# Attention pairs of a fused kernel: raw queries loaded to both halves of the partitions, earlier loads, and another order of sixteen block moves

## The chip, the core and the metric

The program runs on one NeuronCore of one Trainium2 chip. Its time is device microseconds (us) for the whole program, one launch. Three executions of the kernel before gave 1097.83, 1100.74 and 1102.21 us, so the median is 1100.74. The profiled execution took 1099.78 us.

## The reference

Three stages follow each other. Only the first one is touched by the change.

```python
def _attn_ref(q, k, v):                       # 4 batches x 8 heads, S = 1152, D = 64
    q_pool = q.reshape(B, H, S // 2, 2, D).mean(axis=3)      # 576 pooled queries
    scores = scale * np.matmul(q_pool, k.transpose(0, 1, 3, 2))
    scores = scores - np.max(scores, axis=-1, keepdims=True)
    attn = np.exp(scores)
    attn = attn / (np.sum(attn, axis=-1, keepdims=True) + 1e-09)
    return np.matmul(attn, v)
# then _moe_ref  (576 x 512 tokens: w_k 512x1024, w_v 1024x512, w_r 512x512)
# then _moe2_ref (w_theta, w_tok_r, w_tok_i, w_ch)
```

The inputs are float32, except that the weights of the two later stages arrive as float64 and are converted on the chip.

## The kernel before

**Pairs and slots.** The 32 heads are worked off as 16 pairs P of two heads (h = 0 and 1). A pair has nine slots, one for each tile of at most 128 pooled queries against 1152 keys (the fifth tile, called None in the code, takes the last 64 queries of both heads). A slot makes the scores of the tile two slots ahead on TensorE (L304), takes their maximum on VectorE (L325, or L320 by thirds in the first pair), the exponential on ScalarE (L337), turns the result so that keys lie on partitions, and runs a share of the products with the values (L418, called PV below).

**Two cuts of one number.** Scores are formed to nearly float32 accuracy with numbers cut into a high and a low float32r part. GpSimd makes these cuts for the pair after the running one: `k_hi` (kh), four `k_lo` (kl), and for the queries `q_sum`, `q_scale`, `q_hi`, `q_lo` (the sum of two neighbouring queries, the scale 1/16, the high and the low part). TensorE's 128 rows hold key parts of one head: the high part in the head's own 64 partitions and the low part in the other 64. So the query parts of each head must stand in both halves of the partitions. Before, the cut queries of both heads (128 partitions) are moved there by four DMAs from SBUF to SBUF at the end of `q_lo` (L254), into the buffers Q12. The high key part moves by two DMAs (`k_move`, L268).

**Two ways to turn.** For pairs 1 to 14 the first four slots are turned in 32 x 32 blocks on VectorE (`turn_blocks`, L372, into the tile BLK). When the fourth is done, `move_blocks` (L380) puts the blocks in place with sixteen DMAs, from partitions 32a.. of BLK to partitions 32m.. of the tile E. One moves 144 KB. The first PV products that read E run in the eighth slot. The other five slots are turned on TensorE (L347) and copied by ScalarE and VectorE (L403).

**Weight conversion.** Beside this, 20 pieces of float64 weights are converted. A piece is loaded (L123, 512 KB), ScalarE takes a magnitude (L127), GpSimd clamps (L130), VectorE puts bits together in three steps, ScalarE and GpSimd cut (L146, L150), and two DMAs store (L154, L155). With a the slot of the first bit step, the load stands in slot a-6, the magnitude in a-3 and the clamp in a-2.

**What sets the order.** The order on each engine is written out by hand: `at_gap`, `at_mid` and `at` put a step at the start, in the middle or at the end of a slot (hooks 0, 1, 2). The table PREP lists (slot, hook, step, arguments) for the preparation of pair P during pair P-1 (PREP1 for P = 1). Steps whose name begins with l are loads, for pair P+1. All DMAs go out from SyncE's (SP's) queue in program order, so a DMA that waits for something holds up every DMA behind it. The tile pools give buffers in turn and add the waits. Raw queries, raw keys and high key parts have two buffers each (pool nat), E and BLK one.

Of the kernel before, what the change touches and what calls it, by code (L numbers as in the profile page):

```python
# [48 lines left out]
PREP1 = ((-1, 2, 'qs', 'pool'), (1, 0, 'kh', 'pool'), (1, 2, 'km'), (1, 2, 'kl', 'pool', 0, 0), (1, 2, 'kl', 'pool', 0, 1), (2, 2, 'qx', 'pool'), (2, 2, 'qh', 'pool'), (2, 2, 'ql', 'pool'), (3, 2, 'kl', 'pool', 1, 0), (4, 2, 'kl', 'pool', 1, 1), (5, 0, 'lqk'), (15, 2, 'lv'))  # L49
PREP = ((-1, 2, 'qs', 'pool'), (0, 0, 'kh', 'pool'), (0, 1, 'km'), (0, 1, 'qx', 'pool'), (0, 2, 'qh', 'pool'), (1, 1, 'ql', 'pool'), (2, 1, 'kl', 'pool', 0, 0), (3, 1, 'kl', 'pool', 0, 1), (4, 1, 'kl', 'pool', 1, 0), (5, 1, 'kl', 'pool', 1, 1), (7, 0, 'lqk'), (16, 0, 'lv'))  # L50
# [13 lines left out]
def attn_moe_kernel(ctx: ExitStack, tc: tile.TileContext, qT, kT, vP, muk, mur, wk, wv, wr, wth, wtr, wti, wch, ident, out):  # L64
# [94 lines left out]
    def attention(first):  # L159
# [73 lines left out]
        def q_sum(P, e):  # L233
            q = raws[P][0]
            engines[e].tensor_tensor(q[:, 0], q[:, 0], q[:, 1], ALU.add)  # L235

        def q_scale(P, e):
            q = raws[P][0]
            if e == "act":
                act.activation(q[:, 0], q[:, 0], AF.Copy, scale=1.0 / 16.0)  # L240
            else:
                engines[e].tensor_scalar(q[:, 0], q[:, 0], 1.0 / 16.0, 1.0, op0=ALU.mult, op1=ALU.mult)

        def q_hi(P, e):
            q = raws[P][0]
            cut_hi(e, q[:, 1].bitcast(F32R), q[:, 0])

        def q_lo(P, e):
            q = raws[P][0]
            cut_lo(e, q[:, 0], q[:, 0], q[:, 1])  # L250
            Q = Q12[P % 2]
# [3 lines left out]
            for h in range(2):
                d = slice(64 * h, 64 * h + 64)
                c = 512 * (1 - h)
                cut_hi("pool", QC[P % 2][d, d], q[d, 0, c:c + 64])
# [237 lines left out]
        steps = {
            "qs": q_sum, "qx": q_scale, "qh": q_hi, "ql": q_lo, "kh": k_hi, "kl": k_lo, "km": k_move,
            "lqk": load_qk, "lv": load_v,
        }

# [680 lines left out]
```

## Time and profile before

| what | value |
|---|---|
| median of three executions | 1100.74 us |
| profiled execution | 1099.78 us |
| its span, first to last instruction | 1098.0 us |
| pairs 0 to 15 | about 8.7 to 603 us of the span |
| TensorE busy | 957.4 us (87%) |
| VectorE / ScalarE / GpSimd busy | 694.3 / 515.7 / 528.1 us |
| mean granted TensorE clock | 0.941 |
| moved by DMA | 159.20 MB |

The two later stages, from about 603 us on, keep TensorE busy nearly all the time; in the pairs it waits. A view of waits lists an engine and line, what it waited for, the total in us, how often and the longest. A row of the timeline is start, duration, engine, line, operation, output and inputs, count, and in brackets the idle time before it with what ended it. The view of windows gives for each stretch its length, each engine's busy time with its count of instructions, TensorE's granted clock as a share of 2.4 GHz, the mean busy share of the 16 DMA engines and what they moved.

### The profile page before, as it was taken

The numbers are of one execution on the slowest core, as the hardware profiler recorded it, in microseconds if no ns is written. First come the engines' busy times: TensorE is split into PE (matmuls) and PEld (weight loads), VectorE is DVE, ScalarE is ACT, GpSimd is POOL, SyncE is SP. The second block draws the span as 40 slices with busy tenths as digits, with TensorE's granted clock in tenths as the row PEclk, the third lists the DMA queues.
The fourth block names the chain that finished last, engine by engine and source line by source line (L and its number), as shares of the span: only waits on it lengthen the run. The fifth ranks groups of instructions, "written<-read, shape, count | busy, mean of one in ns | idle before, by whom it ended". The sixth has DMA issues, their size and how long they took to land.

```text
span 1098.0 us, 17551 instructions
## 1 busy us (share of the span) xinstructions
PE 957.4 (87%) x6328; PEld 809.4 (74%) x6328; DVE 694.3 (63%) x1006; ACT 515.7 (47%) x1101; POOL 528.1 (48%) x571
## 2 busy tenths in 40 slices
PE   8686985796787687679689999999999999999998
PEld 6554664564555464556457899999999999999998
DVE  7485764675765575575445478888873676366631
ACT  7364444454545454454346555555554444244320
POOL 7415523532542453355135156566654665566641
PEclk9898987897988898898889999999999999999999
DMA  5777768768767777786671923333341240000011
GB/s 156 208 199 191 213 178 205 227 195 204 203 193 222 192 213 204 199 226 167 188 189 66 340 94 107 99 97 93 103 132 64 85 165 17 28 23 23 1 44 44
DMA packets 69927, 159.20 MB, mean 145 GB/s; under 512 B 12176, under 2 KB 31312, under 8 KB 69840
## 3 DMA queue, kind: packets, MB, share of 16 engines
q1 hardware_dynamic: 69840, 158.07, 50.8%
q8 instruction: 50, 0.82, 0.3%
q14 instruction: 37, 0.30, 0.1%
HBM read 73.08 MB, written 24.79 MB: 89 GB/s over the span
## 4 chain that ended last, share of the span: by engine, by line
PE 50%; issue 5%; SPq 4%; DMA 4%; DVE 4%; ACT 2%; POOL 1%; POOLq 0%; ACTq 0%; DVEq 0%
PE ps L1073 10%; PE ps L825 8%; PE ps L806 8%; PE pv L418 5%; PE ps L1092 5%; PE ps L1019 5%; PE sc L304 4%; SPq L380 3%; PE ps L775 2%; PE sc L347 2%; DMA cv<-wv 1%; DMA a<-wk 1%; DMA a<-wth 1%; DVE m L325 1%; PE ps L977 1%
## 5 line engine op out<-in xcount | busy, mean ns | idle before, releaser
L304 PE MATMUL sc<-kt,q 128*128 128x384 f32 (+1 forms) x864 | 214.7, 373 | 74.4 <-ACT M L403 62.5
L325 DVE TENSOR_REDUCE m<-sc 128x1 f32<-128x1152 f32 x138 | 187.1, 1356 | 113.9 <-PE sc L304 107.6
L304 PEld LDWEIGHTS sc<-kt,q 128*128 128x128 f32 (+1 forms) x864 | 151.7, 198 | 108.4 <-ACT M L403 66.1
L337 ACT ACTIVATE e<-sc,m 128x1152 f32<-128x1152 f32 x144 | 176.5, 1226 | 83.7 <-DVE m L325 79.6
L418 PE MATMUL pv<-E,vn 128*64 128x256 f32 x576 | 84.6, 436 | 51.9 <-DMA scr<-rt 50.1
L235 POOL TENSOR_TENSOR qn<-qn 128x576 f32<-128x576 f32 x15 | 21.3, 1417 | 199.5 <-DMA qn<-qT 145.6
L1073 PE MATMUL ps<-b,a 128*128 128x288 f32 x816 | 111.3, 296 | 0.0
L1073 PEld LDWEIGHTS ps<-b,a 128*128 128x128 f32 x816 | 109.4, 188 | 0.6
L403 DVE COPY M<-sc 128x384 f32<-128x384 f32 x77 | 41.8, 546 | 99.8 <-PE sc L347 99.7
L806 PE MATMUL ps<-x,a 128*128 128x288 f32 x768 | 103.7, 295 | 1.0 <-DVE xt L830 1.0
L418 PEld LDWEIGHTS pv<-E,vn 128*64 128x64 f32 x576 | 43.9, 153 | 80.9 <-issue 67.5
L825 PE MATMUL ps<-k,b 128*128 128x288 f32 x768 | 103.5, 295 | 0.0
L806 PEld LDWEIGHTS ps<-x,a 128*128 128x128 f32 x768 | 102.2, 188 | 1.4 <-DVE xt L830 1.3
L825 PEld LDWEIGHTS ps<-k,b 128*128 128x128 f32 x768 | 102.1, 188 | 0.3
L201 POOL TENSOR_TENSOR kt<-kn,kh 64x576 fp32r<-64x576 f32 (+1 forms) x64 | 93.2, 1472 | 3.1
L347 PEld LDWEIGHTS sc<-idn,e 128*128 128x128 f32 x528 | 67.5, 157 | 35.3 <-issue 17.6
L347 PE MATMUL sc<-idn,e 128*128 128x128 f32 x528 | 86.6, 307 | 6.7 <-ACT e L337 5.8
L403 ACT COPY M<-sc 128x384 f32<-128x384 f32 x83 | 39.3, 479 | 108.9 <-PE sc L347 108.5
L418 PE MATMUL pv<-M,vn 128*64 128x320 f32 x576 | 87.5, 440 | 0.0
L372 DVE STREAM_TRANSPOSE blk<-e 128x1152 f32<-128x1152 f32 x56 | 76.6, 1368 | 0.0
L793 POOL TENSOR_TENSOR k<-h,k 128x288 fp32r<-128x288 f32 x64 | 56.7, 901 | 18.7 <-ACT k L792 17.6
L418 PEld LDWEIGHTS pv<-M,vn 128*64 128x64 f32 x576 | 37.3, 136 | 36.1 <-issue 11.3
(136 smaller groups left out, 1604.3 us busy)
## 6 DMA issues: line engine op xcount, KB each, us to landing
E<-blk SPq DMA_DIRECT2D x224, 144.0 KB
q<-qn SPq DMA_DIRECT2D x60, 288.0 KB
vn<-vP SPq DMA_DIRECT2D x16, 576.0 KB
kt<-kh SPq DMA_DIRECT2D x31, 288.0 KB
kn<-kT SPq DMA_DIRECT2D x15, 576.0 KB
qn<-qT SPq DMA_DIRECT2D x15, 576.0 KB
b<-wtk SPq DMA_DIRECT2D x9, 576.0 KB
rb<-scr SPq DMA_DIRECT2D x32, 144.0 KB
```

The lines of the kernel that those rows point to most:

```text
L201: engines[e].tensor_tensor(out, x, hi.bitcast(F32), ALU.subtract)
L304: r = pe.matmul(sc[0:m, c, 0:384], lhsT=x, rhs=k[:, 384 * c:384 * c + 384], start=(i == 0), stop=(i == len(ops) - 1),)
L325: r = dve.tensor_reduce(m, scs[n][:, :, 0:384], axis=AX.XY, op=ALU.max, negate=True)
L337: r = act.activation(e, sc[:, :, 0:384], AF.Exp, bias=m, scale=1.0, accum_out=rss[P][:, t:t + 1])
L347: r = pe.transpose(ps[:, 128 * j:128 * j + 128], es_[n][:, c, 128 * j:128 * j + 128], idn)
L372: dve.transpose(out, es_[n].rearrange("p a b -> p (a b)").rearrange("p (k m i) -> p k m i", k=KT, m=4))
L403: r = (act.copy if e == "act" else dve.tensor_copy)(out, ps)
L418: pe.matmul(out, lhsT=vns[P][:, h, j], rhs=e, start=(x == 0), stop=(x == KT - 1))
L793: pool.tensor_tensor(q[:, 1], h, q[:, 0].bitcast(F32), ALU.subtract)
L806: pe.matmul(ps, lhsT=WK[k, f // 4][:, w, 128 * (f % 4):128 * (f % 4) + 128], rhs=x[k][:, c], start=(k == 0 and n == 0), stop=(k == 3 and n ...
L825: pe.matmul(pss[d], lhsT=WV[f][:, w, 128 * d:128 * d + 128], rhs=k2[f][:, c], start=(f == 0 and n == 0), stop=(f == 7 and n == 2))
L1073: pe.matmul(pss[d], lhsT=zs[j][z][:, 128 * d:128 * d + 128], rhs=WTK[min(j, 8)][:, w, cs], start=(m == 0 and n == 0), stop=(m == 8 and n = ...
```

## The change

The queries are no longer cut once for both heads and moved. The raw queries of one head are loaded from HBM to both halves of the partitions (`load_q`, two DMAs of 288 KB per head), and `q_split` makes sum, scale, high and low part for that head on all 128 partitions, writing straight into Q12. So each of the four GpSimd steps on 128 x 576 runs twice per pair, once per head, and the four moves of a pair go. Keys and queries are loaded by separate steps (lk, lq) at other slots. The first pair's raw queries stand in the then unused BLK. The sixteen block moves take the source quarters in turn instead of four moves from one quarter at a time. A conversion piece is loaded one slot earlier, and its magnitude is taken one slot later.

```diff
-PREP = ((-1, 2, 'qs', 'pool'), (0, 0, 'kh', 'pool'), (0, 1, 'km'), (0, 1, 'qx', 'pool'), (0, 2, 'qh', 'pool'), (1, 1, 'ql', 'pool'), (2, 1, 'kl', 'pool', 0, 0), (3, 1, 'kl', 'pool', 0, 1), (4, 1, 'kl', 'pool', 1, 0), (5, 1, 'kl', 'pool', 1, 1), (7, 0, 'lqk'), (16, 0, 'lv'))
+PREP = ((0, 0, 'kh', 'pool'), (0, 2, 'km'), (0, 2, 'q', 0), (2, 2, 'lk'), (2, 2, 'lq', 0), (2, 1, 'kl', 'pool', 0, 0), (2, 2, 'kl', 'pool', 0, 1), (3, 2, 'q', 1), (5, 1, 'kl', 'pool', 1, 0), (5, 2, 'kl', 'pool', 1, 1), (7, 2, 'lq', 1), (16, 2, 'lv'))
...
-            sp.dma_start(out=k, in_=kT[P])
-            sp.dma_start(out=q, in_=qT[P])
...
+        def load_q(P, h):
+            q = qs[P, h] = nat.tile([128, 2, SP], F32, tag="qn", name="qn")
+            for d in (slice(0, 64), slice(64, 128)):
+                sp.dma_start(out=q[d], in_=qT[P][64 * h:64 * h + 64])
...
-            for h in range(2):
-                for d in (slice(0, 64), slice(64, 128)):
-                    sp.dma_start(out=Q[h][d, :, 64 * h:64 * h + SP].bitcast(F32), in_=q[64 * h:64 * h + 64])
...
+        def q_split(P, h):
+            q = Q12[P % 2][h][:, :, 64 * h:64 * h + SP]
+            x = qs.pop((P, h))
+            t = x[:, 0]
+            pool.tensor_tensor(t, t, x[:, 1], ALU.add)
+            pool.tensor_scalar(t, t, 1.0 / 16.0, 1.0, op0=ALU.mult, op1=ALU.mult)
+            cut_hi("pool", q[:, 1], t)
+            cut_lo("pool", q[:, 0], t, q[:, 1])
+            d = slice(64 * h, 64 * h + 64)
+            c = 512 * (1 - h)
+            cut_hi("pool", QC[P % 2][d, d], q[d, 0, c:c + 64].bitcast(F32))
...
             for a in range(4):
-                for m in range(4):
-                    sp.dma_start(out=E[32 * m:32 * m + 32, a], in_=BLK[32 * a:32 * a + 32, m])
+                for b in range(4):
+                    m = (a + b) % 4
+                    sp.dma_start(out=E[32 * m:32 * m + 32, b], in_=BLK[32 * b:32 * b + 32, m])
...
-            q = nat.tile([128, 2, SP], F32, tag="qn", name="qn")
+            q = BLK[:, 0].rearrange("p (a b) -> p a b", a=2)
...
-            at(a - 6, load)
-            at_mid(a - 3, mag)
+            at(a - 7, load)
+            at_mid(a - 2, mag)
```

SP's queue around the block moves of pair 4, before (kt<-kh is `k_move`, q<-qn the moves of the cut queries, cv a conversion piece, E<-blk the block moves, scr and rb the row sums, vn, kn and qn loads):

```order
L268 DMA kt<-kh 64x1152 x2
L123 DMA cv<-wk 128x1024
L254 DMA q_1_0_125<-qn 64x1152 x2
L254 DMA q_1_1_126<-qn 64x2x576 x2
L154 DMA wk_80<-cv 128x512
L155 DMA wk_80<-cv 128x512
L380 DMA E<-blk 32x1152 x16
L442 DMA scr<-rt 10x32 x4
L449 DMA rb<-scr 64x576 x2
L231 DMA vn<-vP 128x1152
L225 DMA kn<-kT 128x1152
L226 DMA qn<-qT 128x1152
```

The same stretch of SP's queue now:

```order
L255 DMA kt<-kh 64x1152 x2
L154 DMA wk_80<-cv 128x512
L155 DMA wk_80<-cv 128x512
L224 DMA kn<-kT 128x1152
L229 DMA qn<-qT 64x1152 x2
L368 DMA E<-blk 32x1152 x16
L430 DMA scr<-rt 10x32 x4
L123 DMA cv<-wk 128x1024
L437 DMA rb<-scr 64x576 x2
L233 DMA vn<-vP 128x1152
L229 DMA qn<-qT 64x1152 x2
```

The moves of queries are gone from in front of the block moves; the next keys and the first head's raw queries stand there instead, and the second head's raw queries come after the values.

GpSimd's work for one pair, before (qn raw or cut queries, qc the two corners for the None tile, kt the low key parts):

```order
L235 TENSOR_TENSOR qn<-qn 128x576
L198 TENSOR_SCALAR kh<-kn 128x1152
L242 TENSOR_SCALAR qn<-qn 128x576
L455 TENSOR_TENSOR xt_69<-xt_69,rb 128x576
L198 TENSOR_SCALAR qn<-qn 128x576
L201 TENSOR_TENSOR qn<-qn 128x576
L198 TENSOR_SCALAR qc_127<-qn 64x64 x2
L201 TENSOR_TENSOR kt<-kn,kh 64x576 x2
L130 TENSOR_SCALAR cv<-cv 128x512
L201 TENSOR_TENSOR kt<-kn,kh 64x576 x2
```

The same pair on GpSimd now:

```order
L198 TENSOR_SCALAR kh<-kn 128x1152
L443 TENSOR_TENSOR xt_69<-xt_69,rb 128x576
L239 TENSOR_TENSOR qn<-qn 128x576
L240 TENSOR_SCALAR qn<-qn 128x576
L198 TENSOR_SCALAR q_0_0_123<-qn 128x576
L201 TENSOR_TENSOR q_0_0_123<-qn,q_0_0_123 128x576
L198 TENSOR_SCALAR qc_127<-q_0_0_123 64x64
L201 TENSOR_TENSOR kt<-kn,kh 64x576 x2
L239 TENSOR_TENSOR qn<-qn 128x576
L240 TENSOR_SCALAR qn<-qn 128x576
L198 TENSOR_SCALAR q_0_1_124<-qn 128x576
L201 TENSOR_TENSOR q_0_1_124<-qn,q_0_1_124 128x576
```

The high key part, for which `k_move` waits, now comes ahead of all query steps, and the query steps stand there once per head.

ScalarE in the first slots of pair 2, before (L337 the exponentials, L127 the magnitude):

```order
L337 ACTIVATE e,rs_139<-sc_120,m 128x1152
L127 ACTIVATE cv<-cv 128x512
L337 ACTIVATE e,rs_139<-sc_121,m 128x1152
L337 ACTIVATE e,rs_139<-sc_120,m 128x1152
L428 COPY xt_69<-pv 128x320
```

ScalarE there now:

```order
L324 ACTIVATE e,rs_139<-sc_120,m 128x1152
L324 ACTIVATE e,rs_139<-sc_121,m 128x1152
L127 ACTIVATE cv<-cv 128x512
L324 ACTIVATE e,rs_139<-sc_120,m 128x1152
L416 COPY xt_69<-pv 128x320
```

The magnitude has moved behind one more exponential.

## Rows read from the trace of the kernel before

**Rows 1.** Windows cut at pair starts (pairs 0, 1, 2, 11, 13, 14).

```profile
8.70:44.50 35.80, 24.57 (x160) 19.91 (x159) 20.82 (x38) 19.73 (x36) 23.81 (x27) 0.90 0.62 180
44.50:73.90 29.40, 25.16 (x164) 18.17 (x160) 24.16 (x30) 17.39 (x32) 9.90 (x10) 1.00 0.74 178
73.90:113.80 39.90, 29.38 (x174) 20.82 (x172) 23.85 (x27) 18.57 (x35) 17.15 (x16) 0.87 0.77 206
...
425.50:463.20 37.70, 28.07 (x176) 20.05 (x175) 23.84 (x28) 18.61 (x35) 17.17 (x16) 0.91 0.77 212
...
500.20:539.30 39.10, 28.53 (x174) 19.55 (x173) 20.45 (x22) 16.99 (x32) 14.04 (x13) 0.89 0.72 186
539.30:575.40 36.10, 31.08 (x186) 21.48 (x185) 20.49 (x23) 16.58 (x31) 13.42 (x13) 0.89 0.69 182
```

**Rows 2.** View of waits, whole span, all engines: total, times, longest.

```profile
POOL qn L235 <- DMA qn<-qT: 145.6, 11, 23.2
...
PE sc L304 <- ACT M L403: 62.5, 11, 8.2
...
PE pv L418 <- DMA scr<-rt: 50.1, 12, 9.4
```

**Rows 3.** View of waits, the DMA queue's (SP's) own.

```profile
SPq L268 <- POOL kh L198: 125.1, 15, 10.3
...
SPq L254 <- POOL qn L201: 37.9, 15, 4.7
```

**Rows 4.** Timeline of pair 5 around its block moves.

```profile
203.54 1.37 DVE L372 STREAM_TRANSPOSE blk<-e 128x1152 f32<-128x1152 f32 x1
...
205.86 3.50 SPq L254 DMA_DIRECT2D q<-qn  x4
...
212.68 11.38 SPq L380 DMA_DIRECT2D E<-blk  x16
216.48 0.66 ACT L127 ACTIVATE cv<-cv 128x512 f32<-128x512 f32 x1 [6.90 <-issue]
...
217.56 1.65 PE L304 MATMUL sc<-kt,q 128*128 128x384 f32 x4 [6.74 <-ACT M L403]
```

**Rows 5.** Timeline of pair 13, which has no conversion piece to wait for.

```profile
501.43 1.52 PE L418 MATMUL pv<-E,vn 128*64 128x256 f32 x12
...
511.79 1.37 DVE L372 STREAM_TRANSPOSE blk<-e 128x1152 f32<-128x1152 f32 x1
...
521.78 10.79 SPq L380 DMA_DIRECT2D E<-blk  x16
...
535.28 2.83 PE L418 MATMUL pv<-E,vn 128*64 128x256 f32 x12 [9.39 <-DMA scr<-rt]
```

**Rows 6.** Timeline of pair 1: its block moves and the first products behind them.

```profile
58.50 10.21 SPq L380 DMA_DIRECT2D E<-blk  x16
...
71.48 0.87 PE L418 MATMUL pv<-E,vn 128*64 128x256 f32 x6 [2.11 <-DMA scr<-rt]
```

**Rows 7.** Groups of instructions on GpSimd.

```profile
L235 POOL TENSOR_TENSOR qn<-qn 128x576 f32<-128x576 f32 x15 | 21.3, 1417 | 199.5 <-DMA qn<-qT 145.6 <-issue 53.9
L201 POOL TENSOR_TENSOR qn<-qn 128x576 f32<-128x576 f32 x15 | 21.2, 1416 | 0.9
...
L198 POOL TENSOR_SCALAR kh<-kn 128x1152 fp32r<-128x1152 f32 (+1 forms) x16 | 18.1, 1129 | 1.2
...
L198 POOL TENSOR_SCALAR qn<-qn 128x576 fp32r<-128x576 f32 x15 | 10.1, 676 | 0.2
```

**Rows 8.** Windows inside bursts of DMA: block moves (first, second, third), loads (fourth).

```profile
60.50:65.20 4.70, 4.06 (x29) 3.33 (x28) 4.48 (x7) 3.78 (x9) 0.00 (x0) 1.00 0.95 208
65.20:66.30 1.10, 0.60 (x4) 0.28 (x3) 1.03 (x5) 1.10 (x3) 0.00 (x0) 1.00 0.98 298
...
218.00:224.00 6.00, 6.00 (x29) 5.75 (x28) 3.89 (x8) 3.69 (x8) 0.00 (x0) 0.56 0.94 223
232.00:237.00 5.00, 5.00 (x34) 3.27 (x35) 4.93 (x4) 2.79 (x5) 0.00 (x0) 1.00 0.90 357
```

More of the change, by code (lines that the diff above doesn't have):

```diff
@@ L47 @@
 NORM = (14, 2)
[L49 to L50 removed]
+PREP1 = ((1, 0, 'kh', 'pool'), (1, 2, 'km'), (1, 2, 'q', 0), (2, 2, 'kl', 'pool', 0, 0), (2, 2, 'kl', 'pool', 0, 1), (3, 2, 'q', 1), (4, 2, 'kl', 'pool', 1, 0), (4, 2, 'kl', 'pool', 1, 1), (5, 2, 'lk'), (5, 2, 'lq', 0), (7, 2, 'lq', 1), (16, 2, 'lv'))
+PREP = ((0, 0, 'kh', 'pool'), (0, 2, 'km'), (0, 2, 'q', 0), (2, 2, 'lk'), (2, 2, 'lq', 0), (2, 1, 'kl', 'pool', 0, 0), (2, 2, 'kl', 'pool', 0, 1), (3, 2, 'q', 1), (5, 1, 'kl', 'pool', 1, 0), (5, 2, 'kl', 'pool', 1, 1), (7, 2, 'lq', 1), (16, 2, 'lv'))
 CONV = ((4, 1), (5, 1), (6, 1), (7, 1), (8, 1))
@@ L219, in attention, with load_k @@
             pool.memset(XT[b][:, :, 0:1], 0.0)
-        kts, vns, rss, raws = {}, {}, {}, {}
-        def load_qk(P):
-            q = nat.tile([128, 2, SP], F32, tag="qn", name="qn")
-            k = nat.tile([128, S], F32, tag="kn", name="kn")
-            sp.dma_start(out=k, in_=kT[P])
-            sp.dma_start(out=q, in_=qT[P])
-            raws[P] = [q, k]
+        kts, vns, rss, raws, qs = {}, {}, {}, {}, {}
+        def load_k(P):
+            raws[P] = nat.tile([128, S], F32, tag="kn", name="kn")
+            sp.dma_start(out=raws[P], in_=kT[P])
+        def load_q(P, h):
+            q = qs[P, h] = nat.tile([128, 2, SP], F32, tag="qn", name="qn")
+            for d in (slice(0, 64), slice(64, 128)):
+                sp.dma_start(out=q[d], in_=qT[P][64 * h:64 * h + 64])
         def load_v(P):
@@ L231, in load_v @@
             sp.dma_start(out=v, in_=vP[P])
[L233 to L251, printed above, removed]
-            for h in range(2):
-                for d in (slice(0, 64), slice(64, 128)):
-                    sp.dma_start(out=Q[h][d, :, 64 * h:64 * h + SP].bitcast(F32), in_=q[64 * h:64 * h + 64])
[L255 to L258, printed above, removed]
+        def q_split(P, h):
[9 more added lines that the diff above has]
+            cut_hi("pool", QC[P % 2][d, d], q[d, 0, c:c + 64].bitcast(F32))
         def k_hi(P, e):
             khs[P] = nat.tile([128, S], F32R, tag="kh", name="kh")
-            cut_hi(e, khs[P], raws[P][1])
+            cut_hi(e, khs[P], raws[P])
         def k_move(P):
@@ L272, in k_lo @@
             d, o = slice(64 * h, 64 * h + 64), slice(64 - 64 * h, 128 - 64 * h)
-            cut_lo(e, kts[P, h][o, c], raws[P][1][d, c], khs[P][d, c])
+            cut_lo(e, kts[P, h][o, c], raws[P][d, c], khs[P][d, c])
         khs = {}
@@ L494, in run_pv @@
                 pv_part(*k)
[L496 to L499, printed above, removed]
+        steps = {"q": q_split, "kh": k_hi, "kl": k_lo, "km": k_move, "lk": load_k, "lq": load_q, "lv": load_v}
         def prep_sched(P):
@@ L515, in start @@
                 pe.matmul(ps, lhsT=w[:, 0:128], rhs=w[:, 0:384], start=True, stop=True)
-            q = nat.tile([128, 2, SP], F32, tag="qn", name="qn")
+            q = BLK[:, 0].rearrange("p (a b) -> p a b", a=2)
             k = nat.tile([128, S], F32, tag="kn", name="kn")
@@ L519, in start @@
             kt, kt1 = [kp.tile([128, S], F32R, tag="kt", name="kt") for _ in range(2)]
-            raws[0] = [q, k]
             khs[0], kts[0, 0], kts[0, 1] = kh, kt, kt1
@@ L534, in start @@
             load_v(0)
-            load_qk(1)
+            load_k(1)
+            load_q(1, 0)
+            load_q(1, 1)
             Q = Q12[0]
```

## Prediction

> **What bounds the kernel now.** I read the windows per pair first, then the two views of waits, then the timeline of two pairs, then windows inside bursts of DMA.
>
> The pairs come first because the later stages keep TensorE busy and are not touched. Pairs 2 to 14 run from 73.9 to 575.4 us, 501.5 us or 38.6 each, while pair 1 takes 29.4 [rows 1]. In a pair of 38 to 40 us TensorE is busy 28 to 30 (a part of that at half clock: the mean granted clock is 0.87 to 0.91, against 1.00 in pair 1), VectorE 24, ScalarE 18 and GpSimd 17 [rows 1]. So no engine fills a pair; something is waited for.
>
> The view of waits names two stalls of TensorE. Eleven times, 62.5 us in all, it waits for a copy of ScalarE; twelve times, 50.1 us, its products wait for a DMA [rows 2]. The first is ScalarE standing in its order behind the magnitude of a conversion piece: in pair 5 ScalarE sits idle 6.90 us before L127, and TensorE 6.74 us behind it [rows 4]. The label there is "issue", so what is late is not named; the load of that piece is the only thing the magnitude reads. The second is the block moves. The row names the small scr transfer, which is issued just behind them, but what the products read is E.
>
> Both are late for one reason, SP's queue. In pair 5 the last block turn ends at 203.54 + 1.37 = 204.91, and the block moves could go then. They go at 212.68, 7.8 us late, because the moves of the queries stand first, at 205.86, then the conversion load and stores [rows 4]. In pair 13 the turn ends at 513.16, the moves go at 521.78, 8.6 us late, and the products start at 535.28 after 9.39 us of waiting [rows 5]. SP itself waits 125.1 us for the high key part and 37.9 us for the cut queries [rows 3], both made by GpSimd, and GpSimd waits 145.6 us for the raw queries [rows 2], which were loaded less than two slots before.
>
> **The change, part by part.**
>
> Moves of queries, removed. Nothing that waits on the cut queries stands before the block moves any more. What does is: `k_move`, at times a store or a conversion load, the next keys, and the next first-head queries. The last have a wait: their buffer is free once GpSimd has cut the present first head. Until then GpSimd needs 1.13 (high key part) + about 1.4 (normalisation, a tensor operation of that size) + 1.42 + 0.68 + 0.68 + 1.42 = 6.7, with a small corner about 7 us from the start of the pair [rows 7]; the scale is taken like the high part of the same size. The last turn ends 513.16 - 500.20 = 13.0 us after the start of the pair [rows 1, 5]. So SP has 6 us in hand, and I expect the block moves within 0.5 us of the turn. Behind that load on SP stand stores and the block moves, for which TensorE waits.
>
> Block moves. Issued at once they take 10.21 us to issue, and the products start 12.98 us after the first [rows 6]. In pair 13 the products would have started, unstalled, at 535.28 - 9.39 = 525.89, 12.7 us after the turn [rows 5]. So 0.3 to 1 us of waiting is left where 9.39 stood, even at the old rate.
>
> Conversion. Load one slot earlier, magnitude one slot later: two slots, some 6 us, against stalls of at most 8.2 [rows 2]; and the load no longer stands behind the query moves, which take 3.50 us on SP [rows 4]. The wait goes. A new one is possible: a load waits for an older store to land, and one slot now lies between them, not two. That is up to about 3 us on SP, inside the 6 us in hand.
>
> GpSimd's extra steps. Four steps a second time, 1.42 + 0.68 + 0.68 + 1.42 = 4.2 us per pair [rows 7]; GpSimd goes from about 17 us to 21 of 29. It runs beside TensorE and VectorE. If that cover went, only a late clamp would reach the path, by VectorE; I count 1 us in the first pair, whose steps are packed closest, and none later.
>
> DMA traffic. Block moves run at 223 GB/s at a busy share of 0.94, so 237 at full share; whole-tile loads at 357 and 0.90, so 397 [rows 8]. Removed: 4 x 288 KB of moves (1.18 MB, 5.0 us at 237) and the 576 KB load (1.5 us at 397). Added: 1.18 MB of loads into halves, which the trace shows only in other shapes, so bounded by the two rates, 3.0 to 5.0 us. The 2.36 MB of block moves cost 9.9 us now; in the new order between 5.9 and 9.9. Before, a pair has 0.77 x 37.7 = 29.0 us of DMA work [rows 1]; after, 29.0 - 6.5 + (3.0 to 5.0) - (0 to 4.0) = 21.5 to 27.5. That fits into 29, tightly at the upper end. I take the middle, 24.5, because at the one place where consecutive block moves change from the lower to the upper quarters the rate rises from 208 to 298 GB/s [rows 8], and the new order changes after every second move.
>
> The Trainium skill speaks against this part. Its page "SBUF — State Buffer", section "Door 1: The DMA port swizzle (why `[64,N]` ≈ `[32,N]`)", says that partitions 0 to 63 reach 8 of 16 ports, as 0 to 31 do, and the section on two DMAs for both halves says that two concurrent transfers to both halves gained only 6%. The slow block moves agree with the first; the 298 GB/s at the change goes further than the second allows. By the page the block moves and half loads stay at the low rate and the upper end, 27.5, holds, which is the first rival.
>
> Start. Pair 0 loses its own conversion wait (8.2, the longest [rows 2]). Against it stand 1 us for the late clamp and 1 us because 576 KB more are loaded ahead of its key moves (1.5 to 2.5 us by the two rates, partly hidden). Sum -6.2.
>
> Sum. What length do pairs 2 to 14 get? Pair 13 without its wait and with its products at 1.52 instead of 2.83 us (half clock behind the stall) gives 39.1 - 9.39 - 1.31 = 28.4 [rows 1, 5]. Pair 1, measured, has 29.4 with 2.11 us of waiting [rows 1, 6] but no conversion. I take 29.4: 1 us over the stall-free pair for whatever comes late next. 13 x 29.4 = 382.2, that is -119.3 against 501.5. With -6.2 the profiled 1099.78 becomes 974.3; the median lies 0.96 us above that execution, so about 975.
>
> **The rivals.**
>
> DMA becomes the bound (0.18). With 27.5 us of DMA work, and a share over a whole pair of 0.86 (between the 0.77 of a pair and the 0.95 of a burst [rows 1, 8]), a pair takes 32.0. 13 x 32.0 = 416, -85.5 - 6.2: 1008. For it: in bursts the share is already 0.94 to 0.98. Against: between bursts it is low, and the loads now lie there.
>
> The wait for E takes the place of the conversion's (0.12). Pairs 13 and 14, without conversion waits, take 39.1 and 36.1 [rows 1]; at their mean, 37.6, the sum is 13 x 37.6 = 488.8, -12.7 - 6.2: 1081. For it: E is the last to arrive in such pairs. Against: what made it late there were the query moves, and they are gone.
>
> Slower (0.04): GpSimd holds SP. The load of the next first-head queries stands in front of the block moves and waits for GpSimd. Each us that the cut ends later than 13 us after the start of the pair delays E by one; from 13 + (38.6 - 29.4) = 22 us the pair is slower than before. That is where all of GpSimd's 21 us would lie ahead of it, as if it ran a pair behind. At 24 us a pair takes 40.6, 13 x 40.6 = 528: +26, 1126.
>
> No change (0.02): the stalls move by one place, and the time stays within 5 us.
>
> **How the numbers follow.** The forecast has 0.64. Its own range goes from 13 x 28.4 with all 8.2 us of pair 0 (-132.3 - 8.2: 959) to 30.5 us per pair (-105 - 6: 990). To leave out no more than 2 in 10 the range takes in the DMA-bound rival: 957 to 1012. About 0.5% is what a measurement of this kernel tells from no change. Faster: 0.64 + 0.18 + 0.12 = 0.94; within: 0.02; slower: 0.04.
>
> **What would show it.** Right: the products' wait for a DMA and the wait of L304 for ScalarE fall from 112.6 us to under 20 in all; the block moves start within 1 us of the fourth turn; GpSimd's wait for raw queries is nearly gone; the granted clock in the pairs is near 1.00; pairs of 28.5 to 30 us with a DMA share above 0.8. Wrong: block moves that start more than 3 us after the turn (then what SP waits for in front of them is the cause), packets so late that the products wait 3 us or more although the moves were issued in time (DMA bound), or VectorE waiting for the clamp.

## The result, and the profile after

| | before | after |
|---|---|---|
| median | 1100.93 us (runs beside the changed kernel) | 1009.42 us (4 runs, 1004.99 to 1010.17) |
| profiled execution, its span | 1099.78, 1098.0 us | 1010.17, 1008.4 us |
| mean granted TensorE clock | 0.941 | 0.978 |

The ratio is 0.9164, with an interval from 0.9131 to 0.9197. The kernel is 91.5 us faster. The forecast was 975, 34 us too low; 1008 was the price of the first rival, the one in which DMA becomes the bound. The stated range, 957 to 1012, holds the result only because it was widened to take that rival in; the forecast's own range ended at 990.

The windows of after, cut at the starts of pairs 0, 1, 2, 9, 11, 13 and 14 (columns as in [rows 1]), and at the end pairs 2 to 11 as one window:

```profile
8.60:38.60 30.00, 23.58 (x160) 19.68 (x159) 21.24 (x38) 19.89 (x37) 27.07 (x30) 0.94 0.88 235
38.60:67.20 28.60, 25.03 (x163) 18.16 (x160) 24.61 (x30) 17.16 (x31) 16.43 (x16) 1.00 0.63 159
67.20:100.90 33.70, 27.82 (x174) 19.22 (x173) 24.00 (x27) 18.58 (x35) 21.11 (x20) 0.96 0.84 226
295.30:332.10 36.80, 28.61 (x175) 19.59 (x174) 24.81 (x27) 18.07 (x35) 19.45 (x19) 0.89 0.82 202
364.60:397.90 33.30, 28.62 (x174) 19.57 (x173) 23.17 (x27) 18.57 (x36) 21.54 (x20) 0.91 0.85 227
427.70:455.90 28.20, 26.85 (x178) 18.66 (x175) 20.67 (x23) 17.08 (x33) 19.33 (x18) 1.00 0.85 235
455.90:484.80 28.90, 27.71 (x186) 19.23 (x183) 20.52 (x23) 16.57 (x32) 15.80 (x15) 1.00 0.63 157
67.20:397.90 330.70, 280.90 (x1741) 194.68 (x1740) 242.21 (x270) 182.78 (x336) 208.34 (x194) 0.94 0.84 224
```

The same ten pairs of before:

```profile
73.90:463.20 389.30, 296.38 (x1743) 211.85 (x1741) 242.37 (x271) 182.87 (x335) 164.79 (x154) 0.88 0.76 205
```

Pairs 2 to 14 take 484.8 - 67.2 = 417.6 us, 32.1 each; 29.4 was forecast, 38.6 it was [rows 1]. But they are two kinds. Pairs 12 to 14 take 86.9 us together, 29.0 each, as forecast. Pairs 2 to 11, which have one or two loads of conversion pieces beside them, take 33.1 each, at a clock of 0.94. So nearly all of the miss lies in ten pairs. The last two rows give the DMA work of such a pair, share times length: 0.76 x 38.9 = 29.6 us before, 0.84 x 33.1 = 27.8 after (the share has two digits, so each is rounded to 0.2 us; from one execution to another it can differ by more, as a6_z2 shows below).

The view of waits of after (total, times, longest), the row that answers to the third of [rows 2] and three more:

```profile
POOL xt L443 <- DMA rb<-scr: 63.0, 10, 11.4
...
PE pv L406 <- DMA scr<-rt: 27.7, 9, 6.0
...
PE pv L406 <- DMA E<-blk: 3.9, 2, 3.5
...
PE sc L291 <- DMA kt<-kh: 3.6, 1, 3.6
```

TensorE's wait for ScalarE's copies (62.5 us) and GpSimd's for the raw queries (145.6) have no row any more. What is left is the products' wait for E, 27.7 + 3.9 us for 50.1 + 1.8 (the second number is a row of its own, in which the move of E is named). GpSimd now waits for the row sums, off the path, as a later run shows.

SP's queue, which answers to [rows 3]:

```profile
SPq L123 <- DMA wk<-cv: 22.7, 4, 8.6
...
SPq L123 <- DMA wv<-cv: 20.3, 3, 8.9
...
SPq L123 <- DMA wr<-cv: 18.6, 3, 6.9
...
SPq L229 <- POOL q L201: 13.2, 5, 6.5
...
SPq L255 <- POOL kh L198: 10.9, 3, 4.6
```

The 125.1 us behind the high key part are 10.9. In their place SP waits 61.6 us, ten times, in front of a conversion load, until an older piece's store has landed.

What this does is seen in pair 9, the longest (timeline of after; it answers to [rows 4]):

```profile
298.78 0.53 SPq L154 DMA_DIRECT2D wv<-cv  x1
...
299.35 0.54 SPq L155 DMA_DIRECT2D wv<-cv  x1
...
306.88 1.37 DVE L359 STREAM_TRANSPOSE blk<-e 128x1152 f32<-128x1152 f32 x1
...
308.95 0.33 SPq L123 DMA_DIRECT2D cv<-wv  x1
309.33 0.43 SPq L224 DMA_DIRECT2D kn<-kT  x1
309.86 1.13 SPq L229 DMA_DIRECT2D qn<-qT  x2
...
311.10 13.45 SPq L368 DMA_DIRECT2D E<-blk  x16
...
324.72 1.88 SPq L430 DMA_DIRECT2D scr<-rt  x4
...
328.01 2.83 PE L406 MATMUL pv<-E,vn 128*64 128x256 f32 x12 [5.95 <-DMA scr<-rt]
...
328.76 1.74 SPq L437 DMA_DIRECT2D rb<-scr  x2
```

SP stands still from 299.89 to 308.95. The last turn ends at 308.25, the block moves start 2.85 us later, and then their issue takes 13.45 us, not the 10.21 of [rows 6], behind a conversion load, the keys and the queries, 512 + 576 + 2 x 288 KB, which went in within the 2 us ahead. From their start to the products it is 16.9 us. But the transfers do not stand still while SP does, as the window over that stretch shows (share 0.84, 219 GB/s):

```profile
300.00:309.00 9.00, 9.00 (x57) 5.52 (x55) 7.66 (x7) 4.77 (x8) 8.43 (x9) 1.00 0.84 219
```

Pair 13, with no conversion load (timeline; it answers to [rows 5]):

```profile
439.28 1.37 DVE L359 STREAM_TRANSPOSE blk<-e 128x1152 f32<-128x1152 f32 x1
...
440.71 10.31 SPq L368 DMA_DIRECT2D E<-blk  x16
...
453.48 1.52 PE L406 MATMUL pv<-E,vn 128*64 128x256 f32 x12
```

Here the moves start 0.06 us after the turn, products 12.8 us after that, nothing waits, and the pair has 28.2 us for the 28.4 reckoned.

### The profile page after: what moved, and what is told of

Read it like the earlier page. It is cut to its first block, busy times and chain, and to the rows that moved or that the text cites. A ratio compares the mean times of both kernels' runs of the same rounds, so it can differ in the third digit from the quotient of the medians.

```text
span 1008.4 us, 17632 instructions
## 1 busy us (share of the span) xinstructions
PE 935.0 (93%) x6328; PEld 789.0 (78%) x6328; DVE 691.8 (69%) x1006; ACT 517.3 (51%) x1101; POOL 593.0 (59%) x631
## 4 chain that ended last, share of the span: by engine, by line
PE 65%; DMA 13%; DVE 6%; SPq 6%; issue 5%; POOL 3%; ACT 2%; ACTq 0%; POOLq 0%; DVEq 0%
PE ps L1059 11%; PE pv L406 11%; PE sc L291 9%; PE ps L811 9%; PE ps L792 8%; DMA E<-blk 5%; PE ps L1078 5%; PE ps L1005 5%; SPq L368 4%; PE sc L334 3%; PE ps L761 3%; DMA scr<-rt 2%; DMA qn<-qT 2%; DVE m L312 2%; DMA a<-wk 1%
## 5 line engine op out<-in xcount | busy, mean ns | idle before, releaser
L291 PE MATMUL sc<-kt,q 128*128 128x384 f32 (+1 forms) x864 | 204.8, 359 | 25.0 <-DVE M L391 20.3
L291 PEld LDWEIGHTS sc<-kt,q 128*128 128x128 f32 (+1 forms) x864 | 143.1, 188 | 59.2 <-DVE M L391 33.1
L406 PE MATMUL pv<-E,vn 128*64 128x256 f32 x576 | 78.9, 413 | 31.6 <-DMA scr<-rt 27.7
L391 DVE COPY M<-sc 128x384 f32<-128x384 f32 x77 | 41.8, 545 | 72.5 <-PE sc L334 72.4
L201 POOL TENSOR_TENSOR kt<-kn,kh 64x576 fp32r<-64x576 f32 (+1 forms) x64 | 90.1, 1427 | 2.2
L334 PEld LDWEIGHTS sc<-idn,e 128*128 128x128 f32 x528 | 61.3, 147 | 36.5 <-ACT e L324 18.4
L334 PE MATMUL sc<-idn,e 128*128 128x128 f32 x528 | 80.0, 290 | 8.2 <-ACT e L324 7.1
L406 PEld LDWEIGHTS pv<-E,vn 128*64 128x64 f32 x576 | 41.2, 145 | 58.5 <-issue 43.9
L150 POOL TENSOR_TENSOR cv<-cv 128x512 fp32r<-128x512 f32 x20 | 25.6, 1278 | 77.1 <-ACT cv L146 63.5
```

What stands on the lines that cost most here:

```text
L201: engines[e].tensor_tensor(out, x, hi.bitcast(F32), ALU.subtract)
L291: r = pe.matmul(sc[0:m, c, 0:384], lhsT=x, rhs=k[:, 384 * c:384 * c + 384], start=(i == 0), stop=(i == len(ops) - 1),)
L334: r = pe.transpose(ps[:, 128 * j:128 * j + 128], es_[n][:, c, 128 * j:128 * j + 128], idn)
L391: r = (act.copy if e == "act" else dve.tensor_copy)(out, ps)
L406: pe.matmul(out, lhsT=vns[P][:, h, j], rhs=e, start=(x == 0), stop=(x == KT - 1))
```

## The experiments

Each kernel is timed against the kernel before. "Work" is the DMA share times the mean length of pairs 2 to 11, from one window over them as in the rows above (its row stands below where the argument needs it). Pairs, work and waits are those of the one profiled execution, which can lie off the median: 1013.93 us for a6_z2 (8.1 above it), 985.77 for q128 (4.9 below), 1053.77 for before_early (4.4 below). The last column adds the rows of waits that name scr and E.

| kernel | median, us | ratio [interval] | pair 2 to 11, us | share, work us | products' wait for E, us |
|---|---|---|---|---|---|
| after | 1009.42 | 0.9164 [0.9131, 0.9197] | 33.1 | 0.84, 27.8 | 31.6 |
| load_a6 | 1001.59 | 0.9105 [0.9054, 0.9155] | 31.8 | 0.87, 27.7 | 22.5 |
| old_blocks | 1014.41 | 0.9208 [0.9181, 0.9236] | 33.2 | 0.84, 27.9 | 34.7 |
| old_conv | 1005.36 | 0.9137 [0.9108, 0.9166] | 32.0 | 0.87, 27.8 | 26.1 |
| late_loads | 1016.47 | 0.9230 [0.9201, 0.9258] | 33.4 | 0.84, 28.1 | 23.3 |
| before_early | 1058.13 | 0.9637 [0.9601, 0.9674] | 35.6 | 0.85, 30.2 | 67.4 |
| before_conv | 1089.08 | 0.9915 [0.9883, 0.9947] | 38.4 | 0.78, 29.9 | 92.9 |
| before_diag | 1093.36 | 0.9948 [0.9930, 0.9965] | 38.2 | 0.75, 28.7 | 43.6 |
| a6_z2 | 1005.83 | 0.9174 [0.9126, 0.9223] | 33.0 | 0.87, 28.7 | 30.2 |
| q128 | 990.67 | 0.8994 [0.8947, 0.9041] | 30.8 | 0.84, 25.9 | 15.7 |
| more | 1031.29 | 0.9358 [0.9319, 0.9398] | 34.5 | 0.85, 29.4 | 43.6 |
| a6_n_st | 1001.06 | 0.9087 [0.9045, 0.9129] | 32.1 | 0.87, 27.9 | 20.9 |
| best | 983.23 | 0.8936 [0.8901, 0.8971] | 30.6 | 0.84, 25.7 | 14.5 |

Two theories stood against each other after the result. A: SP's queue is held in front of the block moves by the conversion load that waits for a store. B: the transfers themselves are the limit in pairs 2 to 11, as the first rival had it.

**load_a6: the changed kernel with the conversion load a slot later.**

```diff
-            at(a - 7, load)
+            at(a - 6, load)
```

> The changed kernel with the load of a conversion piece back in slot a-6 (the magnitude stays in a-2). Theory A (SP is held: the load waits on SP for an older store to land, 61.6 us in ten waits, up to 9 us, and the next keys, queries and the block moves stand behind it): SP's waits of L123 for stores fall under 20 us, the products' wait for E falls from 27.7 to under 14 us, time 985 to 997. Rival B (the DMA engines are full, share 0.80 to 0.86 in pairs 2 to 11, whatever the order): wait about 28 us, time 1004 to 1012.

SP's wait in front of these loads fell from 61.6 to 41.8 us (17.2 + 12.8 + 11.8), the products' from 31.6 to 22.5, and pairs 2 to 11 by 1.2 us each, but pair 0 grew by 3.2 with a wait of 6.1 us for its keys. 1001.59 lies between the forecasts of A and B, and the intervals of the two kernels overlap; by itself the run separates nothing.

**old_blocks: the changed kernel with the old order of the block moves.**

```diff
-                for b in range(4):
-                    m = (a + b) % 4
-                    sp.dma_start(out=E[32 * m:32 * m + 32, b], in_=BLK[32 * b:32 * b + 32, m])
+                for m in range(4):
+                    sp.dma_start(out=E[32 * m:32 * m + 32, a], in_=BLK[32 * a:32 * a + 32, m])
```

> The changed kernel with the block moves in the old order (four from one quarter, then the next). If the new order helps as the changed kernel's packets say (about 0.57 us per move in a packed stretch against 0.68 before): each E comes 1.5 to 2 us later, the products' wait rises from 27.7 by 12 to 25 us, time 1018 to 1035. If two neighbouring moves gain next to nothing by lying in different halves: 1005 to 1013.

Pairs 2 to 11 as one window:

```profile
70.00:401.80 331.80, 280.71 (x1744) 193.87 (x1742) 240.87 (x271) 182.75 (x336) 208.50 (x194) 0.96 0.84 223
```

Share, rate and length are those of after: 0.84, 223 against 224 GB/s, 331.8 against 330.7 us. The new order saves about 0.1 us of DMA work a pair, which is within the rounding, where 0 to 4.0 stood in the prediction. The median, 1014.41, lies between the two forecasts, 5 us above after's, with overlapping intervals. A small gain of the order is seen in pair 1, where the moves are issued in 10.1 to 10.2 us. Its moves and the products that wait for them, in after and then here:

```profile
52.53 10.13 SPq L368 DMA_DIRECT2D E<-blk  x16
...
64.82 1.52 PE L406 MATMUL pv<-E,vn 128*64 128x256 f32 x12 [0.39 <-DMA E<-blk]
```

```profile
54.67 10.21 SPq L367 DMA_DIRECT2D E<-blk  x16
...
67.59 1.51 PE L405 MATMUL pv<-E,vn 128*64 128x256 f32 x12 [1.01 <-DMA scr<-rt]
```

From the first move to the products it is 12.29 us in the new order and 12.92 in the old, 0.63 less (before had 12.98 [rows 6]).

**old_conv: the changed kernel with the conversion's old slots.**

```diff
-            at(a - 7, load)
-            at_mid(a - 2, mag)
+            at(a - 6, load)
+            at_mid(a - 3, mag)
```

> The changed kernel with the conversion as before (load a-6, magnitude a-3). Theory A: SP's waits of L123 for stores fall as in load_a6; the magnitude comes one slot earlier, so TensorE's wait for ScalarE's copies comes back in part, 0 to 20 us: time 990 to 1010. Rival (the shift of the magnitude was what removed the 62.5 us): that wait is over 40 us and the time 1030 to 1055.

TensorE's wait for ScalarE's copies comes to 1.5 us, at slots that cost 62.5 us before. So it was not the shift that removed it. The time is not told apart from after's.

**late_loads: the changed kernel with the next keys and first-head queries loaded behind the block moves.**

```diff
-PREP = ((0, 0, 'kh', 'pool'), (0, 2, 'km'), (0, 2, 'q', 0), (2, 2, 'lk'), (2, 2, 'lq', 0), (2, 1, 'kl', 'pool', 0, 0), (2, 2, 'kl', 'pool', 0, 1), (3, 2, 'q', 1), (5, 1, 'kl', 'pool', 1, 0), (5, 2, 'kl', 'pool', 1, 1), (7, 2, 'lq', 1), (16, 2, 'lv'))
+PREP = ((0, 0, 'kh', 'pool'), (0, 2, 'km'), (0, 2, 'q', 0), (2, 1, 'kl', 'pool', 0, 0), (2, 2, 'kl', 'pool', 0, 1), (3, 2, 'q', 1), (4, 2, 'lk'), (4, 2, 'lq', 0), (5, 1, 'kl', 'pool', 1, 0), (5, 2, 'kl', 'pool', 1, 1), (7, 2, 'lq', 1), (16, 2, 'lv'))
```

> The changed kernel with the next keys and the first head's raw queries loaded in slot 4, behind the block moves, instead of slot 2 ahead of them. Theory A (1.15 MB in front of E in the queues, and SP late, make E late): the products' wait falls from 27.7 to under 15 us, time 988 to 999. Rival B (DMA engines full): the same bytes in another order, wait 20 to 30, time 1002 to 1012.

The products' wait fell to 18.7 + 4.6 us, but now GpSimd waits for the keys. 1016.47 is above both forecasts. From the view of waits:

```profile
POOL kh L198 <- DMA kn<-kT: 18.7, 4, 6.6
PE pv L406 <- DMA scr<-rt: 18.7, 7, 5.4
```

Work (28.1 for 27.8) and length (33.4 for 33.1) of a pair are nearly the same; the place of the wait moves. That fits B, but a new wait came in with the edit, which may hide a gain.

**before_early: the kernel before, with its keys and queries loaded at the end of slot 2, not at the start of slot 7.**

```diff
-PREP = ((-1, 2, 'qs', 'pool'), (0, 0, 'kh', 'pool'), (0, 1, 'km'), (0, 1, 'qx', 'pool'), (0, 2, 'qh', 'pool'), (1, 1, 'ql', 'pool'), (2, 1, 'kl', 'pool', 0, 0), (3, 1, 'kl', 'pool', 0, 1), (4, 1, 'kl', 'pool', 1, 0), (5, 1, 'kl', 'pool', 1, 1), (7, 0, 'lqk'), (16, 0, 'lv'))
+PREP = ((-1, 2, 'qs', 'pool'), (0, 0, 'kh', 'pool'), (0, 1, 'km'), (0, 1, 'qx', 'pool'), (0, 2, 'qh', 'pool'), (1, 1, 'ql', 'pool'), (2, 1, 'kl', 'pool', 0, 0), (3, 1, 'kl', 'pool', 0, 1), (4, 1, 'kl', 'pool', 1, 0), (2, 2, 'lqk'), (5, 1, 'kl', 'pool', 1, 1), (16, 0, 'lv'))
```

> The kernel before with one edit: the raw keys and queries are loaded in slot 2, half a pair ahead, instead of slot 7; the cut queries are still moved by four DMAs. Theory C (what made the block moves late was the late load: GpSimd's 145.6 us of waiting for raw queries, SP's 125.1 us behind it): GpSimd's wait under 30 us, SP's wait for the high key part under 40, block moves within 3 us of the turn, time 1020 to 1050. Rival D (the query moves themselves stand in front of the block moves and fill the DMA engines): the two stalls of TensorE stay at 80 us or more in all, time 1070 to 1095.

```profile
PE pv L418 <- DMA scr<-rt: 62.9, 10, 9.8
...
POOL qn L235 <- DMA qn<-qT: 16.6, 4, 11.6
...
PE sc L304 <- ACT M L403: 8.5, 4, 7.7
```

Against [rows 2], the raw queries' wait falls from 145.6 to 16.6 and the wait for ScalarE from 62.5 to 8.5, while the products' rises from 50.1 to 62.9. One table entry gives 41.6 us against the 1099.73 of the kernel before beside it, nearly half of the gain, with every query move still in place. The time lies between the forecasts of C and D: the waits of GpSimd and SP fell as C said (SP's for the high key part to 30.5), but block moves still start up to 4.8 us after the turn. Its pairs of 35.6 us with 30.2 us of work have a share of 0.85, as after has.

**before_conv: the kernel before with the conversion's new slots.** The edit is the reverse of old_conv's.

> The kernel before with the conversion's shift alone (load a-7, magnitude a-2). The wait of L304 for ScalarE's copies falls from 62.5 to under 15 us; the products' wait for E takes its place and rises from 50.1 to 85 to 105, time 1080 to 1098. Rival (the two waits are independent): E's wait stays near 50 and the time is 1030 to 1050.

The wait for ScalarE goes entirely, and the products' takes its place: 92.9 us in 14 waits. 10.7 us are gained (1099.73 beside it) of 62.5 removed, and most of that in pair 0, which has no block moves and takes 25.9 us for 35.8; pairs 2 to 11 take 38.4 for 38.9. So the conversion's wait was one of two that covered each other.

**before_diag: the kernel before with the new order of the block moves.** The edit is the reverse of old_blocks'.

> The kernel before with the new order of the sixteen block moves alone. As the other way round cost 5 us: 1092 to 1097, products' wait for E 2 to 8 us shorter in all. If E's packets are not the limit while SP sends them late: 1098 to 1102.

The 6.4 us (1099.73 beside it) are small, but the interval leaves out 1. The work falls from 29.6 to 28.7 us a pair, which is no more than two executions can differ by (see a6_z2); in pair 1 the products start 12.27 us after the first move for 12.98, about the gain that old_blocks gives back.

**a6_z2: load_a6, and the pieces' stores a slot earlier.**

```diff
-            at(z + 3, store)
+            at(z + 2, store)
```

> The changed kernel with the load of a conversion piece back in slot a-6 and its store one slot earlier (z+2 instead of z+3, z the slot of the last bit step), so that one to two more slots lie between a store and the load that waits for it. Theory A (SP is held by that load): SP's waits of L123 for stores fall from 61.6 (41.8 with the load alone) to under 20 us, the products' wait to under 15, time 985 to 997. Rival B (DMA engines): 999 to 1005.

This is the test of A. SP's waits for these stores are gone but for 0.2 us, and the block moves start within 0.1 us of the turn in 12 of 14 pairs. Yet the products wait as before (30.2 us), and pairs 2 to 11 take 33.0 us. Timeline of its pairs 3 and 11, the turns, the block moves and the products:

```profile
118.00 1.37 DVE L359 STREAM_TRANSPOSE blk<-e 128x1152 f32<-128x1152 f32 x1
119.44 10.67 SPq L368 DMA_DIRECT2D E<-blk  x16
...
133.85 1.52 PE L406 MATMUL pv<-E,vn 128*64 128x256 f32 x12
...
376.98 1.37 DVE L359 STREAM_TRANSPOSE blk<-e 128x1152 f32<-128x1152 f32 x1
378.47 15.71 SPq L368 DMA_DIRECT2D E<-blk  x16
...
396.37 2.42 PE L406 MATMUL pv<-E,vn 128*64 128x256 f32 x12 [3.75 <-DMA scr<-rt]
```

Both start 0.1 us after the turn; in pair 3 the sixteen moves take 10.67 us to issue and nothing waits, in pair 11 they take 15.71 and the products wait 3.75. Moves that are issued in time now crawl. So A fails as the main cause: without the hold, the bytes that stood behind it go in front of the block moves or among them. The median, 1005.83, misses A's 985 to 997 and is just above B's 999 to 1005. Two things limit this run. Its profiled execution is the longest of four, so 33.0 us a pair is a high value. And its work, 28.7 us, is 1.0 above load_a6's with the same transfers, so that much can lie between two executions. The other kernels with this load in slot a-6 (load_a6, old_conv, a6_n_st) have pairs of 31.8 to 32.1 us at after's work: up to about 1 us a pair may still be A's.

**q128: the changed kernel with one 128-partition load per head in place of two of 64.** The input holds the queries twice, one copy under the other, so the bytes into the core stay.

```diff
-            for d in (slice(0, 64), slice(64, 128)):
-                sp.dma_start(out=q[d], in_=qT[P][64 * h:64 * h + 64])
+            sp.dma_start(out=q, in_=qD[P][h])
...
+        "qD": c(np.concatenate([turned.transpose(0, 1, 4, 3, 2)] * 2, axis=2)),
```

> Each pair's half of the queries comes in one transfer over all 128 partitions, from an array in HBM that holds the queries twice; the bytes into the chip's memory stay (288 KB for each half of the partitions and each head), and two transfers instead of four are issued a pair. Theory B (the transfer engines are the limit in pairs 2 to 11, and transfers that touch only half of the partitions are the slow ones): the four transfers of 288 KB, some 4.9 us a pair at 240 GB/s, should come to about 3.1 us at the 380 GB/s that the windows show for loads of the whole width, so 1.8 us a pair over ten pairs: 985 to 995 us, and TensorE's wait for the block moves' transfers falls from 27.7 to under 15 us. Rival (only the bytes in front of the block moves count, or their own 16 transfers, not the form of the queries' loads): 1003 to 1010 us, and the wait stays at 20 to 30 us.

```profile
66.40:374.80 308.40, 275.11 (x1744) 190.68 (x1741) 243.44 (x271) 183.08 (x336) 206.49 (x193) 0.98 0.84 239
```

The share stays at 0.84 and the rate goes from 224 to 239 GB/s: the same bytes in 25.9 us of work for 27.8. The pair shortens by 2.2 us in the profiled executions, and the median by 19 us in all, although SP's waits in front of the conversion loads are as in after (22.0 + 19.3 + 18.4 = 59.7). B was expected at 985 to 995. The products' wait is at its edge (15.2 + 0.5).

**more: the changed kernel with 448 KB a pair that nothing reads.**

```diff
+        MORE = ring.tile([128, 896], F32, name="more")
...
+            if h == 0 and P > 1:
+                for d in (slice(0, 64), slice(64, 128)):
+                    sp.dma_start(out=MORE[d], in_=kT[P][0:64, 0:896])
```

> Adds, ahead of each first query load from pair 2 on, two loads of 224 KB each, from HBM to one half of the partitions each, into a tile that nothing reads: 448 KB a pair more. Theory B (the transfer engines are full in pairs 2 to 11): 448 KB at 240 GB/s are 1.9 us a pair, over the ten pairs that have a conversion beside them 19 us, the four others absorb it: 1025 to 1035 us, TensorE's wait for the block moves' transfers rises from 27.7 to 40 us or more. Rival (the transfers have room; the late start of the block moves is due to what SyncE's queue waits for): 1007 to 1015 us, since two issues more (1.1 us of SyncE's queue a pair) are all that is added.

```profile
69.90:415.40 345.50, 285.12 (x1740) 196.95 (x1739) 243.53 (x270) 182.97 (x335) 209.07 (x194) 0.94 0.85 227
```

The edit puts the two loads right behind each first head's query loads, not ahead of them as the expectation says, but still in front of the block moves. 22 us slower, as B had it. The work is up 1.6 us a pair, the pair 1.5. Pairs 12 to 14 did not absorb theirs: 31.1 us each for 29.0. With q128 this is the answer in both directions: take 1.9 us of transfer work out and the pair is 2.2 shorter, put 1.6 in and it is 1.5 longer. No instruction of a compute engine changed in either. What did change beside the transfers is two issues of SP fewer or more, about 1.1 us a pair, less than either change of the pair. Both changes of work stand above the 1.0 that a6_z2 showed, and best below repeats the first (25.7 against 27.9 in a6_n_st).

**a6_n_st: load_a6, GpSimd's division two slots later, pair 1's first queries behind pair 0's key moves.**

```diff
-            at(min(P * KT + o, NT) + (4 if P < NP - 1 else 6), norm2, P)
+            at(min(P * KT + o, NT) + (4 if P == NP - 2 else 6), norm2, P)
...
-            load_q(1, 0)
-            load_q(1, 1)
...
                 sp.dma_start(out=kh[h0].bitcast(F32), in_=kt[h0].bitcast(F32))
+                load_q(1, 0)
+                load_q(1, 1)
```

> Three small moves in the changed kernel: the conversion's load one slot later (as in the first experiment, which took 1001.6 us by itself), GpSimd's division of a pair's outputs two slots later (it waited 63.0 us for the sums' round trip through HBM), and pair 1's query loads of the start behind the key moves of pair 0. Theory (GpSimd has 7 to 9 us of slack in each pair, so its wait costs nothing; the start's query loads cost the 3.6 to 6 us that pair 0's products wait for their keys): 996 to 1000 us, GpSimd's wait for the sums falls below 20 us with no gain from it, pair 0 comes to 29.5 us or less. Rival (GpSimd's wait delays the query splits and so the next pair): below 992 us, with pairs 2 to 11 a microsecond shorter each.

GpSimd's wait for the row sums falls from 63.0 to 13.4 us, and pairs 2 to 11 are no shorter than load_a6's (32.1 against 31.8): the 63.0 us were off the path. Pair 0 takes 25.3 us for load_a6's 33.2, its key wait gone. But the profiled execution as a whole is only 4.0 us shorter and the median the same, while the four runs of either kernel spread over 8 and 13 us; that pair 0's gain is kept to the end is not shown.

**best: q128 and a6_n_st together.**

> The two last edits together, as a candidate for the quickest: the whole-width query loads (990.7 us by themselves) and the three small moves (1001.1 us by themselves, 8 us under the changed kernel, of which pair 0 makes some 4). Theory B (both give back transfer time in front of the block moves, and pair 0's gain is apart from it): pair 0 at 25.3 to 26 us for 28.7, pairs 2 to 11 at 29.5 to 30 us each for 30.8: 978 to 985 us, and TensorE's wait for the block moves' transfers under 10 us. Rival (with the whole-width loads the conversion's place no longer matters): only pair 0's 3 us come, 986 to 990 us.

983.23 us, the quickest measured, 10.6% under the kernel before. Pair 0 takes 25.6 us, pairs 2 to 11 take 30.6, at a clock of 0.99:

```profile
63.20:369.20 306.00, 272.58 (x1743) 188.27 (x1741) 246.55 (x271) 182.96 (x336) 205.91 (x191) 0.99 0.84 243
```

The median falls where B had it, but not by its steps. Pair 0 came (3.1 us under q128's). Pairs 2 to 11 were to take 29.5 to 30 us and take 30.6, 0.2 under q128's, and the products still wait 10.1 + 4.4 us. That q128's and this kernel's intervals overlap leaves open whether the conversion's place is worth anything beside whole-width loads.

## Why the prediction was right, and where it was off

The direction was right, and the waits were the right ones; but the bound that took over is that of the rival given 0.18, not of the forecast given 0.64. That the first rival's 32.0 us a pair meets the 32.1 measured over pairs 2 to 14 is in part luck: the rival has thirteen pairs alike, the kernel has ten of 33.1 and three of 29.0.

**What bounds the kernel before: right for two of the three waits.** Late loads made GpSimd's and ScalarE's waits: before_early takes them from 145.6 and 62.5 us to 16.6 and 8.5 without touching a query move, for 41.6 us. The products' wait is not cured by that, it rises to 67.4. The rest of the change is worth some 49 us on top, 1058.1 to 1009.4: 2.4 us less transfer work a pair and pairs 2.5 us shorter.

**The conversion's wait: gone, but not by the step named.** "Two slots" was the reason given. With the old slots in the changed kernel it stays away (old_conv), and with the new ones in the old kernel the products' wait swallows most of it (before_conv). What freed it is that the load no longer stands behind something late: in before_early 8.5 us of it are left, at the old slots and with every query move in place.

**Block moves at the turn: right in half the pairs.** They start within 0.1 us of it in 7 of 14 pairs and over 1 us late in three (1.8, 2.7 and 2.9 us). "Up to about 3 us on SP" for a load that waits for an older store was too small: single waits reach 8.9 us and exceed the 6 us in hand. By itself that costs at most about 1 us a pair (a6_z2 and the kernels beside it). The prediction also named the sign of a DMA bound, products that wait 3 us or more behind moves issued in time. It is there in pairs 2, 7 and 11: moves 0.79, 0.58 and 0.43 us after the turn, products waiting 3.65, 4.14 and 3.53 us. Pair 7 of after:

```profile
243.54 1.37 DVE L359 STREAM_TRANSPOSE blk<-e 128x1152 f32<-128x1152 f32 x1
...
245.49 13.96 SPq L368 DMA_DIRECT2D E<-blk  x16
...
261.79 2.33 PE L406 MATMUL pv<-E,vn 128*64 128x256 f32 x12 [4.14 <-DMA scr<-rt]
```

**GpSimd: right.** 208.3 / 10 = 20.8 us a pair against 21 reckoned. No wait of VectorE for a late clamp is left in the list. SP does wait for GpSimd's cuts, as the slower rival had it (13.2 us in five waits), but in pairs 0, 1, 12 and 13 alone, and the block moves of the last three start at the turn.

**Pair 0: right in sum.** 29.9 us, 5.9 less, against 6.2. Its parts were off: the key moves cost 3.6 us for 1.

**The step that failed: DMA work per pair, 24.5.** The sum was 29.0 - 6.5 + (3.0 to 5.0) - (0 to 4.0), and the middle was taken. The traces give 27.8 after and 29.6 before. Both open terms came out at their dear ends. The half loads: replacing them with whole-width loads took 1.9 us off the work, which is the 2.0 between 3.0 and 5.0; if whole-width loads cost the 3.0, the half loads had cost the 5.0. The new order: 0.1 us with the changed kernel's loads around it, 0.9 in before_diag, about 0.6 to 0.7 in the burst of pair 1, where the middle put 2.0. With 5.0 and 0 the sum is 27.5, the first rival's work, for 27.8 measured.

The choice rested on one window of 1.1 us at 298 GB/s [rows 8]. A whole burst of the new order shows little of it. Windows of after, pair 1 inside its block moves and pair 9 inside its own:

```profile
53.80:64.20 10.40, 7.48 (x47) 6.01 (x47) 9.55 (x15) 8.19 (x15) 6.16 (x5) 1.00 0.93 225
314.00:324.00 10.00, 5.89 (x35) 4.29 (x34) 9.05 (x13) 6.93 (x13) 3.59 (x4) 0.99 1.02 240
```

At full share that is 225 / 0.93 = 242 and 240 / 1.02 = 235 GB/s, where the old order had 223 / 0.94 = 237 and, in pair 1, 208 / 0.95 = 219 [rows 8]. What moved at 298 in that 1.1 us of before stays open; no run took it apart. The Trainium skill's page "SBUF — State Buffer", in its section "Can I just issue two DMAs to hit both halves?", says that only one transfer over all 128 partitions reaches all 16 ports, and that two transfers at once to both halves gain 6%. The runs agree: the order gained 0.63 of 12.92 us, 5%, and one whole-width load in place of two gained the 1.9 us.

**Why a share of 0.84 is a bound.** Forecast were pairs of 28.5 to 30 us with a share above 0.8; the share came, the pairs did not. Two windows of after's pair 9, up to about the end of the block moves' transfers and behind it, and a row of SP's waits tell why a pair does not reach 1:

```profile
295.30:325.80 30.50, 24.51 (x156) 16.87 (x154) 24.81 (x27) 17.67 (x33) 19.45 (x19) 0.97 0.93 230
325.80:330.00 4.20, 1.99 (x10) 1.37 (x12) 0.00 (x0) 0.00 (x0) 0.00 (x0) 0.50 0.11 27
```

```profile
SPq L437 <- DMA scr<-rt: 21.1, 21, 2.4
```

For 30.5 us the share is 0.93; behind the last block move the transfer engines stand nearly idle for 4.2 us (0.11). In the timeline above, the row sums (scr) go out behind the block moves, rb waits for them and goes at 328.76, and the next loads stand behind it in SP's queue. So the 27.8 us of work must fit into less than the pair. In the table, length less work is 4.1 to 5.4 us for each of the eleven kernels that load keys and first queries by slot 4, whatever their work, and 8.5 to 9.5 for the three that load them in slot 7 (before 38.9 - 29.6 = 9.3). So the change took 4.0 us of idle transfer time out of such a pair and 1.8 us of work. Filling the stretch that is left was not tried. In pairs 12 to 14 there is no conversion load: 0.85 x 28.2 = 24.0 us of work in pair 13, and such a pair ran as forecast.

**Clock.** "Near 1.00" holds in pair 1 and 13 and not in pairs 2 to 11, 0.94. The clock falls to 0.50, 1.2 GHz, behind the products' wait (row 325.80:330.00). TensorE's work in these ten pairs took 280.9 us busy, and 272.6 in best at 0.99; how much of those 8 us is on the path no run shows.

**The sum.** 974.3 was forecast for the profiled execution and 1010.2 came, 35.9 more. Pairs 2 to 14 hold 417.6 - 382.2 = 35.4 of it.

## What to carry to other kernels

Before a gain is added up, reckon the transfer work of a stage in us (share times length), and where a term of it is open, let the dear end stand unless a whole burst shows otherwise; a window of 1 us is no rate. A change that lets a queue run on time also moves its bytes in front of whatever is urgent: ask what then stands ahead of it, in bytes and not only in waits. And two waits at one place cover each other: taking out the larger gave 10.7 us of 62.5, and pairs 2 to 11 only 0.5 us each.
